# One add and one reciprocal per head, key low parts on GpSimd, first q loads on another queue

## The chip, the cores and the metric

The kernel runs on one core of a Trainium2 chip. A core has TensorE (PE, matrix products; its weight loads are shown as PEld), VectorE (DVE), ScalarE (ACT), GpSimd (POOL) and SyncE (SP), which here issues most of the DMA transfers. Each engine works through its own list of instructions in order and waits on semaphores for the others. The metric is the device time of one execution in microseconds; smaller is better.

## The reference

Attention over 4 batches, 8 heads, 576 positions and head size 64, with a mask in blocks of 64, and behind it two feed-forward layers (the second a mixture of four experts). The part that the change touches is the attention:

```python
scores = scale * np.matmul(q, k.transpose(0, 1, 3, 2))
scores = np.where(mask, scores, -1000000000.0)          # block_i >= block_j
scores = scores - np.max(scores, axis=-1, keepdims=True)
attn = np.exp(scores)
attn = attn / (np.sum(attn, axis=-1, keepdims=True) + 1e-09)
out = np.matmul(attn, v)
# then h = max(x @ w1, x @ w2, x @ w3); x = h @ w_out; then the four experts
```

## The kernel before

Heads are worked on in pairs. `load_pair` brings q, k and v of a pair; for pair 0 the transfers of q and k are cut by head, so there are four of them, k and q in turn, all issued by SP. `prep_pair` splits q and k into a rounded high part and a low part: the two 64-partition halves of `kk` hold the high part of the keys and the low part (L122, a subtraction, on VectorE), and the queries are split by L133 (ScalarE) and L135 (VectorE).

`scores(g, grp)` makes the scores of head g in two groups: group 0 holds the query blocks 0, 2 and 3 (columns of 128, 384 and 512), group 1 the block 1 (256 columns) and, in every odd head, block 4 (576 columns) for both heads of the pair. Each block goes through a row minimum from PSUM (L208, VectorE; the scores are negated) and an exponential with row sum (L215, ScalarE). At the end the function puts a closure `normalise` on a list: it adds 1e-9 to the group's sums (L223), takes reciprocals (L224), both on VectorE, and multiplies each block in place on GpSimd (L226). `stage` runs the closures of one stage behind the work of the next. `turn_probs` then transposes the blocks on TensorE (L264), in the order block 3, blocks 2 and 0, block 1, block 4; ScalarE or VectorE copy the result to `eh` (L289, L273), and `values` multiplies with v (L310, L318, L322). The result `xf` of a pair is copied by ScalarE (L327 to L334).

The heads of batch 0 run without anything beside them on TensorE. When they are done, the first layer of batch 0 (L505) fills TensorE between the heads of batch 1, and so on. The weights of that layer are converted by a chain over all engines: ScalarE L429 and L431, GpSimd L436, VectorE L438 and L439, GpSimd L443, ScalarE L85, VectorE L452, and a store L453. The rounded copies of `xf` are L523 (ScalarE) and L524 (VectorE).

The order in which instructions stand on each engine is not that of the Python text: the program is built with a scheduler that runs the instructions through a model of time and moves them, so that any edit in the attention can shift others on every engine.

Of the kernel before, what the change touches and what calls it, by code (L numbers as in the profile page):

```python
# [12 lines left out]
ALU = mybir.AluOpType  # L13
# [11 lines left out]
def program(tc, q, k, v, w123, w_out, probs, e_w1, e_w2, out):  # L25
    nc = tc.nc
# [14 lines left out]
    def f(ap):  # L41
        return ap.bitcast(F32)
# [36 lines left out]
    lo, hi, both = slice(0, 64), slice(64, 128), slice(0, P)  # L79

    QT, QW = 2 * (S - 64), 2 * S + 64
    pairs, heads, later = {}, {}, []
# [6 lines left out]
    def load_pair(g):  # L89
        b, h0 = divmod(2 * g, H)  # L90

        if g % 2:
            raw = ap_.tile([P, 2, 2, S], F32, name="raw", tag="raw")[:]
        else:
            o = (B - 1) * KD * S
            raw = arena[:, o:o + 4 * S].rearrange("p (n h s) -> p n h s", n=2, h=2)
        for hs in ((0, 1), (1, 2)) if g == 0 else ((0, 2),):
            for n, src in ((1, k), (0, q)):
                nc.sync.dma_start(out=raw[:, n, hs[0]:hs[1]], in_=src[b, h0 // 2, :, hs[0]:hs[1]])

        vraw = ap_.tile([P, 5, 2, D], F32, name="vraw", tag="vraw", bufs=4)
        nc.sync.dma_start(out=vraw, in_=v[b, h0 // 2])
        pairs[g] = dict(raw=raw, vraw=vraw)

    def prep_pair(g):


        raw, vraw = pairs[g]["raw"], pairs[g]["vraw"]
        if g < NPAIR and g % 2:

            spare = mp.tile([P, 2 * QW + 2 * S], F32R, name="spare", tag="hh")
            q1, q2 = spare[:, 0:QW], spare[:, QW:2 * QW]
            kk = spare[:, 2 * QW:].rearrange("x (h s) -> x h s", h=2)
        else:
            q1, q2 = (ap_.tile([P, QW], F32R, name=x, tag=x, bufs=1)[:] for x in ("q1", "q2"))
            kk = ap_.tile([P, 2, S], F32R, name="kk", tag="kk", bufs=1)[:]
        for x in (q1, q2):
            nc.gpsimd.memset(x[:, QT + 64:QT + 128].bitcast(U32), 0)

        def keys(hs):  # L120
            (rounded if g else lambda _, to, x: rounded(nc.vector, to, x))(nc.scalar, kk[:, hs], raw[:, 1, hs])
            nc.vector.tensor_tensor(kk[hi, hs], raw[hi, 1, hs], f(kk[hi, hs]), op=ALU.subtract)  # L122

        def queries(hs):
            x = raw[:, 0, hs]
            parts = []
            for to in (q1, q2):
                main = to[:, 0:QT].rearrange("x (h s) -> x h s", h=2)[:, hs]
                tail = to[:, QT:QW].rearrange("x (t s) -> x t s", s=64)[:, 0:3:2][:, hs]
                parts.append((main, tail))  # L130
            srcs = (x[:, :, 0:S - 64], x[:, :, S - 64:S])
            for high, src in zip(parts[0], srcs):
                nc.scalar.activation(high, src, ACTF.Copy, scale=-scale)  # L133
            for high, low, src in zip(*parts, srcs):
                nc.vector.scalar_tensor_tensor(low, src, -scale, f(high), op0=ALU.mult, op1=ALU.subtract)  # L135

        if g == 0:
            for h in range(2):
                keys(slice(h, h + 1))
                queries(slice(h, h + 1))  # L140
            yield
        else:
            keys(slice(0, 2))
            yield
            queries(slice(0, 2))
        pairs[g].update(q1=q1, q2=q2, kk=kk)
        if g < NPAIR:
            return
        vs = ap_.tile([P, 2, 5, P], F32R, name="vs", tag="vs", bufs=2)
        vh = vs[:, :, :, 0:64]  # L150
        src = vraw.rearrange("p j h d -> p h j d")
        rounded(nc.gpsimd, vh, src)
        nc.gpsimd.tensor_tensor(vs[:, :, :, 64:128], src, f(vh), op=ALU.subtract)
        pairs[g]["vs"] = vs

    GROUPS = [
        [("x", 512, [(0, 0, P), (2, P, 384)]), ("x", 512, [(3, 0, 512)])],
        [[("x", 512, [(1, 0, 256)])], [("c", 1024, [(4, 192, 576), (1, 768, 256)])]],  # L160
# [2 lines left out]
    def scores(g, grp):  # L163
# [9 lines left out]
        c0 = 3 * grp  # L173
        sets = []
        for tag, cols, plan in GROUPS[1][h] if grp else GROUPS[0]:
            st = (ps_x if tag == "x" else ps_c).tile([P, cols], F32, name="st", tag=tag)
            sets.append((st, plan))
            for i, o, w in plan:
# [5 lines left out]
                c = 0  # L184
                while c < w:
                    n = min(w - c, 512 - (o + c) % 512)
                    terms = [(part, q0, x) for q0, x in todo for part in ("q1", "q2")]
                    ends = masked and i < 4 and c + n == w
                    for m, (part, q0, x) in enumerate(terms):
                        nc.tensor.matmul(  # L190
                            out=st[:, o + c:o + c + n], lhsT=pair[part][:, q0:q0 + P],
                            rhs=pair["kk"][:, x, c:c + n], start=m == 0, stop=m == len(terms) - 1 and not ends,
                        )
                    if ends:
                        nc.tensor.matmul(
                            out=st[:, o + w - 64:o + w], lhsT=corner, rhs=corner[:, 0:64], start=False, stop=True
                        )
                    c += n
        c = c0
        done = []  # L200
        for st, plan in sets:
# [7 lines left out]
            for col, i, o, w in mine:  # L209
                x = ap_.tile([P, w], F32, name=f"p{i}", tag=f"p{i}", bufs=2 if i == 4 else 3)  # L210
# [7 lines left out]
                )  # L218
                done.append((col, x))

        def normalise():
            cs = slice(c0, c)
            nc.vector.tensor_scalar(sm[:, cs], sm[:, cs], 1e-9, None, op0=ALU.add)  # L223
            nc.vector.reciprocal(sm[:, cs], sm[:, cs])  # L224
            for col, x in done:
                nc.gpsimd.tensor_scalar(x, x, sm[:, col:col + 1], 1.0, op0=ALU.mult, op1=ALU.mult)  # L226

        later.append(normalise)


    BANKS = [
# [366 lines left out]
    for g in range(NG_):  # L598
        prep = iter(())

        n = {0: 2, 2: 3, 4: 4}.get(g) if g < H - 1 else (g + 3) // 2 if g % 2 else None
# [11 lines left out]
        b, n_pair = g // H, n  # L613
# [729 lines left out]
```

## Time and profile before

| what | value |
|---|---|
| time, median of 3 runs | 1251.9 us (1250.62 to 1252.67) |
| the profiled execution | 1249.91 us, span 1248.1 us |
| PE busy | 1211.2 us, 97% |
| DVE busy | 929.7 us, 74% |
| ACT busy | 517.8 us, 41% |
| POOL busy | 357.1 us, 29% |

The shares are averages over stages that differ. TensorE is full through most of the span, but not at its beginning: there VectorE, ScalarE and GpSimd are busier than their averages say. Stretches of time have to be read one by one.

### The profile page before, as it was taken

What the parts mean: (1) busy time and instruction counts of PE and PEld (TensorE: products, weight loads), DVE (VectorE), ACT (ScalarE), POOL (GpSimd) and SP (SyncE); (2) the same over time, 40 slices, a digit from 0 to 9 for tenths busy, and PEclk for the clock granted to TensorE, in tenths of its full rate; (3) what the DMA queues carried; (4) which work ended last, traced back from release to release, by engine and by line L of the source; (5) the groups of instructions that cost most, each with busy time, mean ns of one, the idle gap of its engine ahead of it and who ended that gap; (6) DMA issues with size and microseconds to landing.
All of it is one profiled execution on the core that took longest, in us unless ns stands there. A gap on an engine that the chain in (4) does not pass through costs nothing.

```text
span 1248.1 us, 19730 instructions
## 1 busy us (share of the span) xinstructions
PE 1211.2 (97%) x7417; PEld 1157.8 (93%) x7417; DVE 929.7 (74%) x1716; ACT 517.8 (41%) x1076; POOL 357.1 (29%) x444
## 2 busy tenths in 40 slices
PE   7879998999999999999999999999999999999998
PEld 5669997999999999989999998999999999999998
DVE  7978988666565634377888896758787888686896
ACT  7977767544544421233444441233232223322222
POOL 3957786454344212243333341000000000000000
PEclk9999999999999999999999999999999999999999
DMA  8745574554533488478887864778888887776754
GB/s 304 248 164 197 170 265 161 172 153 155 183 102 119 120 287 304 150 303 332 312 311 296 310 247 162 287 274 316 300 306 311 315 314 281 253 258 228 253 210 170
DMA packets 82644, 299.69 MB, mean 240 GB/s; under 512 B 8748, under 2 KB 18036, under 8 KB 69492
## 3 DMA queue, kind: packets, MB, share of 16 engines
q1 hardware_dynamic: 82548, 298.42, 67.3%
q8 instruction: 59, 0.97, 0.3%
q14 instruction: 37, 0.30, 0.1%
HBM read 215.26 MB, written 83.14 MB: 239 GB/s over the span
## 4 chain that ended last, share of the span: by engine, by line
PE 74%; DVE 10%; DMA 5%; POOL 4%; ACT 3%; issue 3%; SPq 0%; DVEq 0%; ACTq 0%; POOLq 0%
PE m L858 24%; PE m L505 19%; PE o L1017 17%; PE st L190 3%; PE pv L359 2%; PE o L940 2%; PE o L943 2%; PE o L944 2%; DMA t<-in_e_w 2%; PE m L1017 2%; POOL p L226 2%; PE tt L264 2%; DVE mn L208 2%; DMA part<-in_e_w 1%; POOL arena L443 1%
## 5 line engine op out<-in xcount | busy, mean ns | idle before, releaser
L505 PE MATMUL m<-xh,wt 128*128 128x288 f32 x1120 | 238.4, 298 | 0.7 <-ACT mt L541 0.4
L858 PE MATMUL m<-t,w 128*128 128x384 f32 x1152 | 228.5, 336 | 0.0
L1017 PE MATMUL o<-hx,w 128*128 128x384 f32 x1176 | 225.7, 337 | 0.0
L1017 PEld LDWEIGHTS o<-hx,w 128*128 128x128 f32 x1176 | 207.8, 188 | 0.1
L858 PEld LDWEIGHTS m<-t,w 128*128 128x128 f32 x1152 | 203.4, 188 | 2.5 <-DVE tmp L878 0.4
L505 PEld LDWEIGHTS m<-xh,wt 128*128 128x128 f32 x1120 | 183.7, 188 | 1.6 <-DVE mt L543 0.8
L858 PE MATMUL m<-b,w 128*128 128x384 f32 x864 | 175.7, 337 | 2.0 <-ACT tmp L883 2.0
L505 PE MATMUL m<-xl,wt 128*128 128x288 f32 x560 | 165.3, 295 | 0.0
L858 PEld LDWEIGHTS m<-b,w 128*128 128x128 f32 x864 | 153.2, 188 | 5.1 <-ACT tmp L883 2.3
L226 POOL TENSOR_SCALAR p<-p,sm 128x128 f32<-128x128 f32 (+1 forms) x144 | 98.7, 702 | 52.1 <-DVE sm L223 17.0
L505 PEld LDWEIGHTS m<-xl,wt 128*128 128x128 f32 x560 | 105.3, 188 | 0.3
L878 DVE TENSOR_TENSOR tmp<-m,tmp 128x384 f32<-128x384 f32 x144 | 77.9, 550 | 19.4 <-PE m L858 19.2
L505 PE MATMUL m<-hh,wo 128*128 128x288 f32 x384 | 81.3, 299 | 2.9 <-ACT arena L554 1.3
L215 ACT ACTIVATE p<-st,mn 128x128 f32<-128x128 f32 (+3 forms) x144 | 78.5, 555 | 8.2 <-DVE mn L208 6.3
L988 ACT CAST hx<-hq 128x768 fp32r<-128x768 f32 x49 | 40.6, 837 | 99.0 <-PE o L1017 75.9
L190 PE MATMUL st<-kk,q 128*128 128x128 f32 (+4 forms) x336 | 71.2, 340 | 8.7 <-ACT q L133 5.5
L940 PE MATMUL o<-w,hh 128*128 128x512 f32 x192 | 74.7, 391 | 0.9 <-ACT hh L918 0.6
L813 POOL TENSOR_TENSOR w<-part,w 128x512 fp32r<-128x512 f32 x32 | 49.2, 1557 | 91.3 <-ACT w L811 61.2
L943 PE MATMUL o<-w,hh 128*128 128x512 f32 x192 | 74.7, 390 | 0.0
L944 PE MATMUL o<-w,hl 128*128 128x512 f32 x192 | 74.1, 390 | 0.0
L543 DVE TENSOR_TENSOR mt<-m,mt 128x288 f32<-128x288 f32 x96 | 43.2, 452 | 40.3 <-PE m L505 39.9
L264 PE MATMUL tt<-ident,p 128*128 128x128 f32 x400 | 61.0, 278 | 9.8 <-POOL p L226 5.4
(169 smaller groups left out, 2173.8 us busy)
## 6 DMA issues: line engine op xcount, KB each, us to landing
w<-kb SPq DMA_DIRECT2D x55, 1024.0 KB, 6.1
w<-ka SPq DMA_DIRECT2D x30, 1792.0 KB, 7.9
ka<-w SPq DMA_DIRECT2D x16, 1792.0 KB, 6.7
wt<-held SPq DMA_DIRECT2D x54, 512.0 KB, 4.1
kb<-part SPq DMA_DIRECT2D x16, 1024.0 KB, 7.0
kb<-w SPq DMA_DIRECT2D x16, 768.0 KB, 4.7
arena<-in_w SPq DMA_DIRECT2D x18, 512.0 KB, 4.0
wo<-held SPq DMA_DIRECT2D x12, 768.0 KB, 4.5
```

The costliest lines, as they stand in the source:

```text
L190: nc.tensor.matmul(out=st[:, o + c:o + c + n], lhsT=pair[part][:, q0:q0 + P], rhs=pair["kk"][:, x, c:c + n], start=m == 0, stop=m == len(t ...
L215: nc.scalar.activation(x, st[:, o:o + w], ACTF.Exp, bias=mn[:, col:col + 1], scale=-1.0, accum_out=sm[:, col:col + 1],)
L226: nc.gpsimd.tensor_scalar(x, x, sm[:, col:col + 1], 1.0, op0=ALU.mult, op1=ALU.mult)
L264: nc.tensor.transpose(tt[:, c:c + P], pt[i][:, k0:k0 + P], ident)
L505: nc.tensor.matmul(out=out_, lhsT=w, rhs=x, start=m == 0, stop=m == n - 1)
L813: eng.tensor_tensor(w[:, a:b, 1], raw[:, a:b], f(w[:, a:b, 0]), op=ALU.subtract)
L858: ins = nc.tensor.matmul(out=m, lhsT=a, rhs=b, start=start and n == 0, stop=stop and n == 3 * KH - 1, skip_group_check=True,)
L878: nc.vector.tensor_tensor(t, x, y, op=ALU.add)
L940: ins = nc.tensor.matmul(out=o, lhsT=hh[:, ts], rhs=wh, start=i == 0, stop=False)
L943: nc.tensor.matmul(out=o, lhsT=hh[:, ts], rhs=wl, start=False, stop=False)
L944: nc.tensor.matmul(out=o, lhsT=hl[:, ts], rhs=wh, start=False, stop=i == G - 1)
L1017: nc.tensor.matmul(out=o, lhsT=a, rhs=b, start=start and m == 0, stop=stop and m == 2, skip_group_check=True,)
```

## The change

Three edits. The q transfers of pair 0 are issued by ScalarE instead of SP. The low parts of the keys of batch 0 (pairs 0 to 3, without the first head) are subtracted on GpSimd instead of VectorE. And a head's groups are normalised together: one add and one reciprocal over all of its sums, behind its second group, and the blocks are multiplied in the order in which they are transposed (3, 2, 0, then 1 or 4). The last edit holds for all 32 heads: 32 adds and 32 reciprocals go.

```diff
         for hs in ((0, 1), (1, 2)) if g == 0 else ((0, 2),):
             for n, src in ((1, k), (0, q)):
-                nc.sync.dma_start(out=raw[:, n, hs[0]:hs[1]], in_=src[b, h0 // 2, :, hs[0]:hs[1]])
+                (nc.sync if g or n else nc.scalar).dma_start(
+                    out=raw[:, n, hs[0]:hs[1]], in_=src[b, h0 // 2, :, hs[0]:hs[1]]
+                )
...
         def keys(hs):
             (rounded if g else lambda _, to, x: rounded(nc.vector, to, x))(nc.scalar, kk[:, hs], raw[:, 1, hs])
-            nc.vector.tensor_tensor(kk[hi, hs], raw[hi, 1, hs], f(kk[hi, hs]), op=ALU.subtract)
+            (nc.gpsimd if g < 4 and hs != slice(0, 1) else nc.vector).tensor_tensor(
+                kk[hi, hs], raw[hi, 1, hs], f(kk[hi, hs]), op=ALU.subtract
+            )
...
+    TURN = (2, 1, 0, 3, 4)
...
+        done = heads[g].setdefault("done", []) + done
+        heads[g]["done"] = done
+
         def normalise():
-            cs = slice(c0, c)
+            cs = slice(0, c)
             nc.vector.tensor_scalar(sm[:, cs], sm[:, cs], 1e-9, None, op0=ALU.add)
             nc.vector.reciprocal(sm[:, cs], sm[:, cs])
-            for col, x in done:
+            for col, x in sorted(done, key=lambda x: TURN.index(x[0])):
                 nc.gpsimd.tensor_scalar(x, x, sm[:, col:col + 1], 1.0, op0=ALU.mult, op1=ALU.mult)

-        later.append(normalise)
+        if grp:
+            later.append(normalise)
```

In the changed program the lines behind the edits have other numbers: L122 is L124, L190 is L195, L226 is L234, L264 is L273, L310 and L318 are L319 and L327, L436 is L445.

GpSimd at the start of the program, before (`kk` and `spare` are keys, `p` the blocks of exponentials, `arena` weights being converted):

```order
L118 MEMSET spare 128x64
L118 MEMSET q_312 128x64
L118 MEMSET q_313 128x64
L226 TENSOR_SCALAR p_167<-p_167,sm 128x128
L226 TENSOR_SCALAR p_169<-p_169,sm 128x384
L226 TENSOR_SCALAR p_172<-p_172,sm 128x512
L226 TENSOR_SCALAR p_179<-p_179,sm 128x256
L436 TENSOR_SCALAR arena<-arena 128x512
```

Head 0's multiplications came first there, in the order of the blocks; the same place in the changed program:

```order
L120 MEMSET spare 128x64
L124 TENSOR_TENSOR kk<-arena,kk 64x576
L124 TENSOR_TENSOR spare<-raw,spare 64x1152
L234 TENSOR_SCALAR p_172<-p_172,sm 128x512
L234 TENSOR_SCALAR p_169<-p_169,sm 128x384
L234 TENSOR_SCALAR p_167<-p_167,sm 128x128
L234 TENSOR_SCALAR p_179<-p_179,sm 128x256
L120 MEMSET q_303 128x64
L120 MEMSET q_304 128x64
L445 TENSOR_SCALAR arena<-arena 128x512
```

The low parts of pairs 0 and 1 now stand ahead of head 0's multiplications, and block 3 (512 columns) comes first among these.

GpSimd later, between pair 1 and pair 3, in the changed program (before, no subtraction of keys stood there):

```order
L445 TENSOR_SCALAR arena<-arena 128x512
L452 TENSOR_TENSOR arena<-arena 128x512
L124 TENSOR_TENSOR kk<-arena,kk 64x1152
L452 TENSOR_TENSOR arena<-arena 128x512
L120 MEMSET spare 128x64
L120 MEMSET spare 128x64
L234 TENSOR_SCALAR p_281<-p_281,sm 128x512
L234 TENSOR_SCALAR p_278<-p_278,sm 128x384
L234 TENSOR_SCALAR p_276<-p_276,sm 128x128
L234 TENSOR_SCALAR p_301<-p_301,sm 128x256
L124 TENSOR_TENSOR spare<-raw,spare 64x1152
L234 TENSOR_SCALAR p_382<-p_382,sm 128x512
```

The subtractions of pairs 2 and 3 stand around head 2's multiplications and ahead of head 3's.

TensorE at the end of batch 0, before: the last product of head 7 with v (`pv_903`) and the transposes of head 8 (`p_805` is its block 3, `p_802` and `p_800` its blocks 2 and 0):

```order
L310 MATMUL pv_902<-eh,vraw 128x128
L264 MATMUL tt<-ident,p_738 128x128 x2
L264 MATMUL tt<-ident,p_805 128x128 x4
L318 MATMUL pv_903<-eh,vraw 128x512 x2
L318 MATMUL pv_903<-eh,vraw 128x384
L318 MATMUL pv_903<-eh,vraw 128x256
L322 MATMUL pv_903<-eh,vraw 128x128
L264 MATMUL tt<-ident,p_802 128x128
L264 MATMUL tt<-ident,p_800 128x128
L264 MATMUL tt<-ident,p_802 128x128 x2
```

Four transposes stood ahead of the product and four behind it; in the changed program (`p_789`, `p_786`, `p_784` are the same blocks) it reads:

```order
L319 MATMUL pv_882<-eh,vraw 128x128
L273 MATMUL tt<-ident,p_724 128x128 x2
L273 MATMUL tt<-ident,p_789 128x128 x4
L273 MATMUL tt<-ident,p_786 128x128
L273 MATMUL tt<-ident,p_784 128x128
L273 MATMUL tt<-ident,p_786 128x128 x2
L327 MATMUL pv_883<-eh,vraw 128x512 x2
L327 MATMUL pv_883<-eh,vraw 128x384
L327 MATMUL pv_883<-eh,vraw 128x256
```

All eight transposes of these blocks now stand ahead of head 7's product.

## Rows read from the trace of the kernel before

**Rows 1.** The page: the span, and TensorE's busy time and share.

```profile
span 1248.1 us, 19730 instructions
...
PE 1211.2 (97%) x7417; PEld 1157.8 (93%) x7417; DVE 929.7 (74%) x1716; ACT 517.8 (41%) x1076; POOL 357.1 (29%) x444
```

**Rows 2.** Windows: length, busy us of each engine, TensorE clock, DMA, GB/s.

```profile
0.00:89.00 89.00, 69.23 (x373) 52.25 (x374) 71.98 (x144) 72.89 (x190) 58.84 (x86) 0.94 0.70 247
89.00:190.00 101.00, 99.02 (x731) 94.05 (x730) 91.76 (x202) 71.81 (x170) 79.19 (x96) 1.00 0.61 203
190.00:230.00 40.00, 34.79 (x239) 31.67 (x239) 31.21 (x78) 28.73 (x74) 24.82 (x37) 1.00 0.52 176
```

**Rows 3.** Chain of waits, 0 to 100 us: start, us, what.

```profile
11.41 1.35 DVE spare L122
...
19.96 1.50 DVE kk L122
...
31.03 2.33 DVE spare L122
...
44.55 2.29 POOL p L226 x4
```

**Rows 4.** Timeline of the first 8 us: start, us, engine, line, what, idle before.

```profile
2.12 0.43 SPq L99 DMA_DIRECT2D arena<-in_q  x1
...
4.13 0.46 DVE L87 TENSOR_SCALAR kk<-arena 128x576 fp32r<-128x576 f32 x1 [4.13 <-DMA arena<-in_k]
...
7.06 0.78 ACT L133 ACTIVATE q<-arena 128x512 fp32r<-128x512 f32 x2 [1.43 <-DMA arena<-in_q]
```

**Rows 5.** VectorE by line and shape, 0 to 100 us: busy us, mean ns.

```profile
L122 DVE TENSOR_TENSOR kk<-arena,kk 64x576 fp32r<-64x576 f32 x2 | 1.5, 755 | 0.1
...
L223 DVE TENSOR_SCALAR sm<-sm 128x1 f32<-128x1 f32 x6 | 0.8, 135 | 0.0
...
L224 DVE RECIPROCAL sm<-sm 128x1 f32<-128x1 f32 x5 | 0.8, 151 | 0.1
```

**Rows 6.** GpSimd by line and shape, whole span.

```profile
L813 POOL TENSOR_TENSOR w<-part,w 128x512 fp32r<-128x512 f32 x32 | 49.2, 1557 | 91.3 <-ACT w L811 61.2 <-PE m L858 18.7 <-PE o L944 11.4
...
L153 POOL TENSOR_TENSOR vs<-vraw,vs 128x640 fp32r<-128x640 f32 x12 | 19.4, 1617 | 0.4
```

**Rows 7.** Timeline of GpSimd and VectorE, 10 to 71 us.

```profile
16.21 2.06 POOL L226 TENSOR_SCALAR p<-p,sm 128x128 f32<-128x128 f32 x4 [2.00 <-ACT p L215]
...
30.55 1.59 POOL L443 TENSOR_TENSOR arena<-arena 128x512 int32<-128x512 int32 x1
...
31.03 2.33 DVE L122 TENSOR_TENSOR spare<-raw,spare 64x1152 fp32r<-64x1152 f32 x1
...
39.45 1.68 POOL L153 TENSOR_TENSOR vs<-vraw,vs 128x640 fp32r<-128x640 f32 x1
...
39.64 2.10 DVE L524 TENSOR_TENSOR xl<-xf,xh 128x576 fp32r<-128x576 f32 x1
...
70.46 0.76 DVE L524 TENSOR_TENSOR xl<-xf,xh 128x576 fp32r<-128x576 f32 x1 [0.69 <-ACT xh L523]
```

**Rows 8.** Timeline from 63 to 89 us, the end of batch 0.

```profile
63.24 2.96 PE L318 MATMUL pv<-eh,vraw 128*128 128x512 f32 x8
...
78.25 0.16 DVE L224 RECIPROCAL sm<-sm 128x3 f32<-128x3 f32 x1
...
78.62 2.70 POOL L226 TENSOR_SCALAR p<-p,sm 128x128 f32<-128x128 f32 x3 [1.95 <-ACT wo L85]
...
81.38 0.66 PE L264 MATMUL tt<-ident,p 128*128 128x128 f32 x4 [4.35 <-POOL p L226]
81.87 4.66 PE L318 MATMUL pv<-eh,vraw 128*128 128x512 f32 x8
...
89.00 0.38 PE L505 MATMUL m<-xh,wt 128*128 128x288 f32 x1
```

**Rows 9.** A window of 10 us, columns as in Rows 2.

```profile
80.00:90.00 10.00, 8.62 (x42) 6.21 (x43) 6.36 (x11) 6.41 (x17) 7.92 (x10) 0.83 0.65 240
```

## The prediction

> **What bounds the kernel now.** I read the page first [rows 1]. TensorE is busy for 1211.2 of 1248.1 us, so all its idle time together is 36.9 us, and no edit here takes a product away from it. The windows say where this idle time lies [rows 2]: 19.8 us (89 less 69.23) in the first 89 us, where the heads of batch 0 run alone until L505's first product [rows 8], 2.0 us from 89 to 190 us and 5.2 us from 190 to 230 us. The other 9.9 us lie behind, where the attention matters little. So the change is worth what it does to the first 89 us, and a little of the 7.2 us up to 230 us.
>
> In the first 89 us no engine is the bound alone: ScalarE is busy for 72.89 us, VectorE for 71.98, GpSimd for 58.84 [rows 2]. The chain of waits shows the turns [rows 3]: up to about 42 us it goes mostly over VectorE, with three subtractions of keys of 1.35, 1.50 and 2.33 us on it; from 44.55 us it goes over GpSimd's multiplications. It ends at the last heads, where TensorE waits 4.35 us for GpSimd at 77.0 us [rows 8].
>
> VectorE and GpSimd are not independent there. The same subtraction of 64x1152 took 1.35 us at 11.41 [rows 3], while GpSimd was still waiting for its first multiplication [rows 7], and 2.33 us at 31.03, where GpSimd's L443 ran from 30.55 to 32.14 [rows 7]. L524 took 0.76 us at 70.46 and 2.10 us at 39.64, where L153 ran until 41.13 [rows 7]. In both cases VectorE's instruction ends as if it had begun when GpSimd's was done.
>
> **The change part by part.**
>
> *The q transfers.* The last q transfer is issued at 2.12 us and ScalarE takes it up at 7.06 [rows 4]; that is where the chain begins. With the k transfers on SP and the q transfers on ScalarE, second place instead of fourth on its queue, it is issued two issues of 0.43 us earlier [rows 4]: at best -0.9 us. On ScalarE nothing but a table load stands behind them, and then work that waits for these very data. But the four transfers share the same DMA engines, and the first k, which VectorE takes up at 4.13 [rows 4], now has company from the start: I bound the loss at +0.3 and take -0.5. The Trainium skill, "DMA: Bandwidth & Descriptors", section on queues, rings and completion order, says that a DMA engine takes turns between the queues it has work for. By that rule the first k and the first q would land together, the first k later than now, and the term would be near 0; no row of before shows two queues. SP's later issues (v and pair 1) move up by the same slots, which is also company for the second q.
>
> *One add and one reciprocal.* Per head one pair of small instructions goes. Where GpSimd leaves VectorE alone the pair costs 0.135 + 0.151 = 0.29 us [rows 5]. For 8 heads this is 2.3 us of VectorE in the first 89 us, and 7 us more spread over the other 24. None of it is on TensorE's path by itself, since ScalarE is as busy as VectorE; I count 0, with 0 and -2.3 as ends. Its other side is a wait: block 3 of a head is no longer multiplied after its own group, but after both. In steady running the scores are made two heads ahead, which hides this.
>
> *The low parts of the keys.* VectorE loses 0.755 us (the second head of pair 0, [rows 5]) and 1.35, 1.50, 2.33 us [rows 3], together 5.9 us. GpSimd gains four subtractions. For them there is no row; L153 gives 1.617 us for 640 columns, 2.53 ns a column, so 1152 columns would be 2.9 us and 576 columns 1.45 us; L813 with 1557 ns for 512 columns is the upper end, 3.5 us [rows 6]. If 64 partitions cost half of 128, the lower end is 1.5 us. I take 2.9, the nearest in form. The first two (1.45 + 2.9) stand ahead of head 0's multiplications, which began at 16.21 after idle time [rows 7]: pair 1's can begin when its rounding ends, at 11.4, and is done at about 14.3, so GpSimd's idle time hides them. The other two, 5.8 us, fall between 20 and 36 us, into a stretch where each engine is busy. VectorE gets 3.83 us back there (1.50 + 2.33). The difference is 2.0 us; VectorE can go on with row minima from PSUM meanwhile, so I take half, +1.0. The ends: -3.8, if GpSimd hides all and VectorE was the bound, and +3.8 (the third rival).
>
> *The order of the multiplications.* At 78.25 the last reciprocal for head 8's first group begins, and GpSimd then does three multiplications in 2.70 us, block 3 as the last; TensorE's four transposes at 81.38 wait for that one [rows 8]. Now block 3 comes first, so these four can start about 1.8 us earlier. But the four transposes of blocks 2 and 0 now also stand ahead of head 7's product, and need the other two multiplications; the product itself so starts hardly earlier, only with 0.66 us less behind it, and I count 1.0. The reciprocal, too, stands closer behind its add: in the changed order one row minimum lies between the two, which I put at 1.0 us earlier. Together -2.0; ends 0 (both eaten by the wait for the second group's sums) and -4.35 (the whole wait).
>
> *The clock behind that wait.* TensorE idled for the 4.35 us. From 80 to 90 us the granted clock is 0.83 of full [rows 9], that is partly at 1.2 GHz, and eight products of head 7 took 4.66 us at 81.87, where those of an earlier head took 2.96 at 63.24 [rows 8]. A shorter wait may spare these 1.7 us; I take a third, -0.6, ends 0 and -1.7.
>
> *Behind 89 us.* VectorE is busy for 91.76 of 101 us from 89 to 190 [rows 2]; 0.29 us less a head gives it air, and the changed order shifts the 7.2 us of TensorE's idle time either way. I take -0.8, ends -2.5 and +2.5.
>
> The sum: -0.5 + 0 + 1.0 - 2.0 - 0.6 - 0.8 = -2.9 us. The profiled execution took 1249.9 us (span 1248.1 and 1.8 around it), which becomes 1247.0; it lies 2.0 below the median of the runs, 1251.9. From the median, I forecast 1249.0 us.
>
> **The rivals.**
>
> *More goes than I count.* Without the whole wait of 4.35 us, the 1.7 us of slow clock and the 0.9 us at the start the gain is 6.95 us: 1245.0. For it speaks that these lie behind one another on the chain; against it that the merged add makes block 3 wait for the second group.
>
> *ScalarE hides it.* ScalarE is busy for 72.89 of 89 us [rows 2], none of its computing goes, and it is in no step of the change but for two issues. If it sets the pace of batch 0, VectorE's free time turns into waiting, and only the first transfers remain: -0.5, so 1251.4. Against it speaks that the chain before 42 us goes over VectorE.
>
> *GpSimd becomes the bound: slower.* By the two pairs of rows above, a subtraction that runs on GpSimd for 2.9 us does not run beside VectorE's work on SBUF; it stops it. Then 5.8 us more of GpSimd push all that follows on its list, head 3's multiplications and the chain from 44.55 us on. The only idle time that could take it up, and that does not itself wait for VectorE, is about 2.0 us, as long as the wait at 16.21 [rows 7]. The price is +3.8: 1255.7. It decides from the point where GpSimd works without a break from pair 2's subtraction to head 5's multiplications. The Trainium skill states this mechanism in "SBUF — State Buffer", section "Who interferes with whom": VectorE with two SBUF inputs and GpSimd take turns on a shared pair of ports, and the one that comes second waits for the whole instruction. The trace agrees with 2.33 against 1.35 us. Against this rival speaks that VectorE's own subtractions, 3.8 us here, stopped GpSimd in the same way before, and that two of the four new ones fall into idle time.
>
> **How the numbers follow.** The forecast has 42 in 100, with 1247 to 1250.5 as its own range; more than I count 12; ScalarE hides it 26; GpSimd as the bound 20. About 0.2%, 2.5 us, is what a measurement of this kernel can tell from no change: faster means below 1249.4, slower above 1254.4. Of the forecast's 42 some 6 lie above 1249.4, so faster has 36 + 12 = 48; the same has 6 + 24 = 30; slower has 20 and 2 from the spread of the second rival, 22. The range reaches from the first rival's time, half a microsecond below, to the third's, a little short of it: 1244.5 to 1255.5.
>
> **What would show it.** At the start, ScalarE's second work on q before 7.06 us. GpSimd's subtraction of 64x1152 at about 2.9 us, and VectorE instructions of 2 us and more beside it, but head 0's multiplications not later than 16.2. The first product of L505, now at 89.00 us [rows 8], some 2 us earlier, the wait at 77 us about half as long, and the clock in the 10 us behind it above 0.83. I am wrong if L505 starts at 89 or later: at the same time with ScalarE without gaps, or later with GpSimd without gaps from 20 to 55 us. I am also wrong if L505 starts earlier and TensorE's idle time from 89 to 230 us grows by as much.

## The result, and the profile after

The changed kernel takes 1260.65 us (median of 6 runs, 1257.64 to 1262.32), the kernel before 1252.79 us in the same series (1250.62 to 1253.97). The ratio is 1.0063, 95% interval 1.0052 to 1.0074: 7.9 us slower, where 1249.0 was forecast, and beyond the upper end of the range, 1255.5. The profiled execution after took 1261.76 us.

The page of the changed kernel, first its span, then busy time and share of each engine:

```profile
span 1260.0 us, 19678 instructions
...
PE 1219.0 (97%) x7417; PEld 1163.9 (92%) x7417; DVE 924.8 (73%) x1648; ACT 516.4 (41%) x1076; POOL 359.7 (29%) x448
```

Against [rows 1] VectorE has 68 instructions fewer and GpSimd 4 more, as the change says. Their busy times (4.9 us less, 2.6 more) do not show by themselves what was moved, since other instructions changed with it: the four subtractions take 9.8 us on GpSimd, its multiplications 3.9 us less than before. TensorE, which has the same 7417 products, is busy 7.8 us longer; its mean granted clock is 0.991 there, 0.996 in the kernel before. The same windows as [rows 2], columns as there:

```profile
0.00:89.00 89.00, 68.49 (x353) 50.64 (x354) 67.90 (x117) 69.87 (x182) 63.90 (x84) 0.96 0.66 225
89.00:190.00 101.00, 98.06 (x725) 93.15 (x724) 89.27 (x181) 70.85 (x167) 75.20 (x100) 1.00 0.63 211
190.00:230.00 40.00, 34.46 (x213) 31.11 (x213) 33.54 (x75) 29.68 (x77) 26.50 (x33) 0.91 0.49 159
```

In each of them TensorE gets through fewer products than before. From 190 to 230 us it is busy for about as long, but at a granted clock of 0.91 instead of 1.00, and does 213 instead of 239. To see where the time went, the span is cut at four products that both kernels have. Each kernel was profiled twice, in us:

```
                              before          after         mean after - before
to the first of L505 (L514)   89.00  90.27    91.15  90.00     +0.9
to the first of L858 (L867)  430.05 429.99   435.69 435.71     +5.7
to the first of L1017        273.60 273.76   277.96 276.47     +3.5
the rest                     455.43 457.12   455.17 455.39     -1.0
span                        1248.1  1251.1   1260.0 1257.6     +9.2
```

The first 89 us, to which the prediction gave nearly all its terms, hold 0.9 of the 9.2 us. The second and the third row repeat within 0.1 and 1.5 us from one execution to the next; the loss is in the program, not in one bad run. It is idle time of TensorE and slower work at once. From the first product of L505 to the first of L858, before and then after:

```profile
89.00:519.05 430.05, 420.73 (x3110) 409.35 (x3109) 284.62 (x680) 218.15 (x530) 204.37 (x294) 1.00 0.55 180
91.15:526.85 435.70, 424.24 (x3114) 412.60 (x3114) 282.12 (x636) 218.43 (x532) 201.68 (x298) 0.99 0.55 181
```

TensorE's idle time grew from 9.3 to 11.5 us; the other 3.5 of the 5.7 us it was busy longer with the same products, at a lower granted clock. In the next stage idle time grew from 2.9 to 4.3 us and busy time from 270.7 to 273.6. In both stages together that is 3.6 us of idle time and 6.4 of slower work; between the second profiles it is 3.1 and 5.3. TensorE's waits in the first of these stages (line, waited for, us in total, times, longest): the first four after, then the first three ahead of L505 before:

```profile
PE m L514 <- ACT wo L85: 2.6, 3, 1.7
PE m L514 <- ACT arena L563: 1.9, 2, 1.3
PE m L514 <- ACT mt L550: 1.6, 3, 0.8
PE m L514 <- DVE mt L552: 1.5, 2, 1.2
```

```profile
PE m L505 <- ACT arena L554: 1.3, 1, 1.3
PE m L505 <- ACT wo L85: 1.0, 2, 0.8
PE m L505 <- ACT mt L541: 0.4, 1, 0.4
```

All waits ahead of products of L505 grew from 3.9 to 8.7 us, and those ahead of the attention's own products fell from 5.4 to 2.8, in both pairs of profiles. None of more than 0.15 us is for GpSimd's multiplications, in either kernel. Two places show how the loss comes about.

**The end of batch 1.** GpSimd, ScalarE and TensorE of the changed kernel (start, us, engine, line, what, idle before and who ended it):

```profile
189.22 0.37 ACT L220 ACTIVATE p<-st,mn 128x128 f32<-128x128 f32 x1
...
193.77 1.31 POOL L452 TENSOR_TENSOR arena<-arena 128x384 int32<-128x384 int32 x1
...
195.11 0.54 ACT L440 ACTIVATE arena<-arena 128x384 int32<-128x384 uint32 x1 [2.69 <-POOL arena L452]
195.56 0.50 ACT L85 CAST wo<-arena 128x384 fp32r<-128x384 f32 x1
...
196.11 0.40 PE L514 MATMUL m<-hh,wo 128*128 128x288 f32 x1 [1.72 <-ACT wo L85]
```

TensorE wants the next rounded piece of `wo`, ScalarE rounds it at 195.56, and ScalarE in turn waited 2.69 us for GpSimd's L452, one step of the same conversion. In the kernel before this conversion was about one piece further on:

```profile
185.23 0.37 ACT L215 ACTIVATE p<-st,mn 128x128 f32<-128x128 f32 x1
...
187.26 0.50 ACT L85 CAST wo<-arena 128x384 fp32r<-128x384 f32 x1
...
190.82 0.55 ACT L431 ACTIVATE arena<-arena 128x384 int32<-128x384 uint32 x1 [1.54 <-POOL arena L443]
191.27 0.50 ACT L85 CAST wo<-arena 128x384 fp32r<-128x384 f32 x1
```

There pieces of `wo` followed 2.0 and 6.0 us behind the head's first exponential (185.23); in the changed kernel the first of them comes 6.3 us behind it (189.22). TensorE's wait for it was 0.2 us before. The wait is followed by a fall of the clock, and so is a later one (0.84 us, for an exponential, at 218.57). The kernel before has waits here too, up to 1.33 us (at 198.1, for a copy to `eh`), and no fall. Windows of 10 us of the changed kernel, then the first of them of the kernel before:

```profile
190.00:200.00 10.00, 7.97 (x45) 6.88 (x45) 8.17 (x19) 7.30 (x20) 8.11 (x9) 0.85 0.51 159
220.00:230.00 10.00, 8.91 (x52) 8.24 (x52) 7.72 (x18) 8.32 (x22) 3.17 (x7) 0.83 0.37 128
```

```profile
190.00:200.00 10.00, 7.87 (x49) 6.65 (x50) 8.05 (x17) 8.65 (x23) 8.50 (x12) 1.00 0.31 97
```

A mean of 0.83 over 10 us means 1.7 us of lost full clock. The second profile of the changed kernel has the same wait of 1.72 us, and 0.83 from 190 to 200 us.

**The experts, behind the attention.** The same products at the same place, before and then after:

```profile
758.07 1.32 PE L858 MATMUL m<-b,w 128*128 128x384 f32 x6 [1.97 <-ACT tmp L883]
759.22 0.39 PE L940 MATMUL o<-w,hh 128*128 128x512 f32 x1
```

```profile
760.36 1.34 PE L867 MATMUL m<-t,w 128*128 128x384 f32 x6 [0.50 <-DVE tmp L887]
...
767.69 2.29 PE L867 MATMUL m<-b,w 128*128 128x384 f32 x6 [2.87 <-ACT tmp L892]
769.77 0.63 PE L949 MATMUL o<-w,hh 128*128 128x512 f32 x1
```

The granted clock there, in windows of 10 us of the changed kernel (1.00 in both in the kernel before):

```profile
760.00:770.00 10.00, 6.77 (x31) 6.46 (x32) 8.98 (x12) 3.60 (x7) 3.25 (x2) 0.85 0.59 188
770.00:780.00 10.00, 10.00 (x41) 8.60 (x41) 4.41 (x7) 0.00 (x0) 0.00 (x0) 0.81 0.24 55
```

The wait grew from 1.97 to 2.87 us, another of 0.50 us came ahead of it, and behind it the same six products took 2.29 instead of 1.32 us, and one of 512 columns 0.63 instead of 0.39: by the granted clock above, TensorE ran at 1.2 instead of 2.4 GHz for part of these 20 us. Nothing of the attention is left on TensorE there, and the change touches no line of it.

**The start.** The places of [rows 4], and GpSimd's first subtraction:

```profile
0.73 0.90 ACTq L99 DMA_DIRECT2D arena<-in_q  x2
0.74 0.87 SPq L99 DMA_DIRECT2D arena<-in_k  x2
...
5.37 0.46 DVE L87 TENSOR_SCALAR kk<-arena 128x576 fp32r<-128x576 f32 x1 [5.37 <-DMA arena<-in_k]
...
6.96 0.78 ACT L137 ACTIVATE q<-arena 128x512 fp32r<-128x512 f32 x2 [0.62 <-DMA arena<-in_q]
...
7.63 2.17 DVE L139 SCALAR_TENSOR_TENSOR q<-arena,q 128x64 fp32r<-128x64 f32 x3
7.86 1.86 POOL L124 TENSOR_TENSOR kk<-arena,kk 64x576 fp32r<-64x576 f32 x1 [6.04 <-DVE q L139]
```

The first k is taken up 1.24 us later than in [rows 4], while the last q comes only 0.10 us earlier. TensorE's first product begins at 6.77 instead of 5.54. In all profiles of this study the first k is taken up at 4.81 to 5.54 with the q loads on ScalarE's queue and at 3.54 to 4.15 without, and TensorE begins at 6.20 to 6.94 and at 5.01 to 5.57.

**The end of batch 0.** TensorE's waits in the first 91 us of the changed kernel (engine, line, waited for, us in total, times, longest):

```profile
PE st L195 <- DVE kk L124: 6.8, 1, 6.8
PE tt L273 <- DVE eh L298: 5.7, 3, 3.3
PE tt L273 <- POOL p L234: 4.5, 5, 1.5
```

The wait of 4.35 us for GpSimd [rows 8] has gone: the longest for a multiplication is 1.5 us. But all waits of the transposes for multiplications together fell only from 5.4 to 4.5 us, and TensorE now waits 5.7 us for VectorE's copies to `eh` ahead of transposes, in the kernel before 1.1 us.

### The profile page after: what moved, and what is told of

It is laid out like the page before. It is cut to its first block, busy times and chain, and to the rows that moved or that the text cites. A ratio compares the mean times of both kernels' runs of the same rounds, so it can differ in the third digit from the quotient of the medians.

```text
span 1260.0 us, 19678 instructions
## 1 busy us (share of the span) xinstructions
PE 1219.0 (97%) x7417; PEld 1163.9 (92%) x7417; DVE 924.8 (73%) x1648; ACT 516.4 (41%) x1076; POOL 359.7 (29%) x448
## 4 chain that ended last, share of the span: by engine, by line
PE 69%; DVE 12%; DMA 6%; ACT 4%; POOL 4%; issue 3%; SPq 0%; ACTq 0%; DVEq 0%; POOLq 0%
PE m L867 21%; PE m L514 18%; PE o L1026 16%; DMA t<-in_e_w 3%; PE st L195 3%; PE pv L368 2%; PE tt L273 2%; PE m L1026 2%; POOL p L234 2%; DVE mn L213 1%; DMA part<-in_e_w 1%; PE o L949 1%; PE o L952 1%; PE o L953 1%; DMA kb<-part 1%
## 5 line engine op out<-in xcount | busy, mean ns | idle before, releaser
L234 POOL TENSOR_SCALAR p<-p,sm 128x512 f32<-128x512 f32 (+2 forms) x144 | 94.6, 675 | 45.3 <-DVE sm L232 23.9
L514 PE MATMUL m<-hh,wo 128*128 128x288 f32 x384 | 84.4, 306 | 5.6 <-ACT wo L85 2.6
L195 PE MATMUL st<-kk,q 128*128 128x128 f32 (+4 forms) x336 | 70.4, 338 | 8.9 <-DVE kk L124 7.4
L273 PE MATMUL tt<-ident,p 128*128 128x128 f32 x400 | 62.3, 280 | 12.5 <-DVE eh L298 5.7
```

What stands on the lines that cost most here:

```text
L195: nc.tensor.matmul(out=st[:, o + c:o + c + n], lhsT=pair[part][:, q0:q0 + P], rhs=pair["kk"][:, x, c:c + n], start=m == 0, stop=m == len(t ...
L273: nc.tensor.transpose(tt[:, c:c + P], pt[i][:, k0:k0 + P], ident)
L514: nc.tensor.matmul(out=out_, lhsT=w, rhs=x, start=m == 0, stop=m == n - 1)
```

## The experiments

All times are medians, each ratio is to the kernel before on the same chip. The stages are those of the table above, read in each kernel's profile. "wo" is TensorE's wait for ScalarE's rounding of `wo` at one product, the 85th of L505 that takes `wo` (at 196.11 us in the changed kernel).

```
                       median   ratio  95% interval        to L505  to L858  to L1017   wo
changed kernel        1260.65  1.0063 [1.0052, 1.0074]     91.15   435.7    278.0     1.72
e1  q only            1257.18  1.0030 [1.0016, 1.0044]     98.10   431.4    273.9      -
e2  keys only         1253.93  1.0013 [1.0002, 1.0024]     91.72   427.9    274.2      -
e3  merge only        1255.67  1.0022 [1.0013, 1.0032]     90.31   432.0    275.2     1.72
e4  keys + merge      1259.90  1.0053 [1.0041, 1.0065]     90.84   435.6    278.0     1.72
e5  q + merge         1261.75  1.0071 [1.0055, 1.0087]     95.81   432.7    277.1      *
e6  q + keys          1254.25  1.0010 [0.9997, 1.0024]     91.08   429.2    275.6      -
k2  keys, 2 pairs     1253.53  1.0008 [0.9997, 1.0019]     91.77   430.2    273.6       -
o1  order only        1254.50  1.0011 [1.0001, 1.0022]     91.36   429.6    275.1       -
m0  merge, heads 0-7  1255.55  1.0023 [1.0012, 1.0033]     93.96   430.4    273.9       -
m1  merge, 8-31       1254.96  1.0013 [1.0003, 1.0023]     90.42   432.9    275.3     1.71
m3  m1 without TURN   1254.84  1.0016 [1.0005, 1.0027]     87.92   434.9    275.6     1.71
d2  no add, 8-31      1251.80  0.9996 [0.9987, 1.0005]     87.93   431.9    275.3      -
d1  one more add      1255.59  1.0018 [1.0009, 1.0027]     90.73   432.7    275.0      -
d3  no add, 0-31      1255.22  1.0017 [1.0007, 1.0027]     91.16   432.8    275.1      -
* 1.6 us for VectorE's low part of wo (L459) at another product; - no wait
```

The intervals are 1.1 to 2.0 us to either side, so a difference of two rows is uncertain by some 2 us. Each stage is read in one execution, which took between 3.0 us less (e2) and 4.2 us more (e1) than its kernel's median. In the two kernels that were profiled twice the stages repeat within 1.7 us, the one up to L858 within 0.1.

**Which of the three edits? One at a time.** The theory after the first comparison was that the late first keys and the merge cost; the rival was GpSimd as the bound.

e1, the q loads alone:

```diff
-                nc.sync.dma_start(out=raw[:, n, ...], in_=...)
+                (nc.sync if g or n else nc.scalar).dma_start(out=raw[:, n, ...], in_=...)
```

> The kernel before with the q transfers of pair 0 on ScalarE's queue alone. Theory A (the two queues share the DMA engines, so the first keys land later): VectorE takes up the first keys at about 5.4 us instead of 4.13, TensorE's first scores end at about 7.2 instead of 6.0, the loss is at least partly kept: +1.2 us (+0.5 to +2). Rival B (the loss of the change comes from the merged normalisation; the start is made up for later): the first keys as late, but the time within 0.5 us of before. Rival C (any edit makes the scheduler deal the instructions out anew, and that decides): 2 us or more to either side, with the instructions of batch 0 and 1 in another order.

e2, the keys alone:

```diff
-            nc.vector.tensor_tensor(kk[hi, hs], ...)
+            (nc.gpsimd if g < 4 and hs != slice(0, 1) else nc.vector).tensor_tensor(kk[hi, hs], ...)
```

> The kernel before with the low parts of batch 0's keys on GpSimd alone. Theory A (a subtraction on GpSimd takes about 3.3 us for 64x1152 and stops VectorE's instructions with two SBUF inputs meanwhile): +1 to +2 us, L505's first product at 90 to 91 us. Rival B (merged normalisation): within 1 us of before, or faster by up to 2, since VectorE is freed of 5.9 us. Rival C (the new order): beyond 2 us to either side.

e3, the merged normalisation with its order, alone:

```diff
+        done = heads[g].setdefault("done", []) + done
+        heads[g]["done"] = done
-            cs = slice(c0, c)
+            cs = slice(0, c)
-        later.append(normalise)
+        if grp:
+            later.append(normalise)
```

> The kernel before with one add and one reciprocal per head, and the multiplications in the order of the transposes, alone. Theory A (start and GpSimd cause the loss): -1 to +2 us. Rival B (a head's first three blocks now wait for its second group, which makes TensorE wait and its clock fall): +4 to +6 us, most of it between 90 and 235 us, with clock falls there that the kernel before does not have. Rival C (new order): beyond 2 us to either side, with no wait that names the sums or the multiplications.

The three cost 4.3, 1.0 and 2.8 us (here and below, differences of medians; the kernel before 1252.9). No single edit gains. In e1 the first keys are taken up late, as in the changed kernel, where e3 has them early:

```profile
5.12 0.46 DVE L87 TENSOR_SCALAR kk<-arena 128x576 fp32r<-128x576 f32 x1 [5.12 <-DMA arena<-in_k]
5.30 0.78 ACT L135 ACTIVATE q<-arena 128x512 fp32r<-128x512 f32 x2 [2.36 <-DMA arena<-in_q]
```

```profile
3.60 0.46 DVE L87 TENSOR_SCALAR kk<-arena 128x576 fp32r<-128x576 f32 x1 [3.60 <-DMA arena<-in_k]
4.33 0.78 ACT L133 ACTIVATE q<-arena 128x512 fp32r<-128x512 f32 x2 [2.31 <-DMA arena<-in_q]
```

In e1 k and q of head 0 are taken up 0.18 us apart instead of 0.73, the k 1.5 us later. The Trainium skill, "DMA: Bandwidth & Descriptors", section on queues, rings and completion order, says that a DMA engine takes turns between the queues it has work for; the traces agree, with these 0.18 us.

**Do they add? Two at a time.** e4, e5 and e6 are the changed kernel with one edit taken back, by the diffs above reversed.

> The changed kernel with the q transfers of pair 0 back on SP; the two other edits stay. Theory A: first keys at 4.1 us again, 1.2 us faster than the changed kernel at the start, and about +6 to +7 us against the kernel before instead of +7.9. Rival B: the same, since the start is a small part under it too; the pair that tells A from B is the keys alone against the merge alone. Rival C (new order): the time moves by 3 us or more against the changed kernel, to either side.

> The changed kernel with all low parts of the keys on VectorE again (q loads on ScalarE's queue and the merged normalisation stay). If the costs of the edits add (alone they cost +4.2, +1.2 and +2.8 us on the means), this is 1252.7 + 7.0 = 1259.7, ratio 1.0056, and the first product of L514 comes near 92 us, its start late by the first keys (VectorE takes them up near 5.2 us instead of 4.13). If the q loads cost only what they add to keys and merge (1260.65 less 1259.90 = 0.8 us), it is 1256.5, ratio 1.0030. If GpSimd with the four subtractions is what makes the merge dear (the first 89-us stage and the one behind it), it is at most 1256, and the time from the first product of L514 to the first of L867 is 433 us or less, against 435.7 in the changed kernel.

> The changed kernel with an add and a reciprocal per group again, in the order of before (q loads on ScalarE's queue and low parts on GpSimd stay). If the costs add: 1252.7 + 4.2 + 1.2 = 1258.1, ratio 1.0043, and the time from the first product of L505 to the first of L858 stays near before's 430 us, with the loss ahead of 89 us. If merge and keys are dear only together, this is near 1256.5 to 1257.2 (ratio 1.0030 to 1.0035), that is q alone. If q's loss is given back when VectorE is relieved of the keys, it is 1254 to 1255.

They do not add. The three single costs make 8.1 us, close to the 7.8 of the changed kernel (here 1260.65 less 1252.9), but only because the misses of the pairs cancel. The merge costs 2.8 us alone, but 6.0 with keys (e4 less e2), 4.6 with q (e5 less e1) and 6.4 with both (the changed kernel less e6). The q loads cost 4.3 and 6.1 us where the keys' low parts stay on VectorE (e1; e5 less e3), and 0.3 and 0.8 us where GpSimd takes them (e6 less e2; the changed kernel less e4). The keys cost 1.0 alone and 4.2 beside the merge (e4 less e3), but win 1.1 and 2.9 us beside the q loads (the changed kernel less e5; e6 less e1): 0.3 on average, which is nothing by these intervals. The merge is the only edit that costs more than the uncertainty in all four places. The rival, GpSimd as the bound, falls with e5: with the keys back on VectorE the kernel is not faster than the changed one. Nor does the loss of e4 over e3 lie where that rival has it: to L505 they differ by 0.5 us, from there to L858 by 3.6. The price of one subtraction was nearly right: 2.64 us in e2 for 1152 columns (2.9 were estimated). The two engines collide as said: the L139 group of three takes 2.17 us beside GpSimd's subtraction, where the kernel before did the same three in 0.22 and 0.83 us, and GpSimd's 576 columns take 1.86 instead of 1.41 us:

```profile
L122 POOL TENSOR_TENSOR spare<-raw,spare 64x1152 fp32r<-64x1152 f32 x2 | 5.3, 2640 | 3.7 <-ACT spare L85 3.6
...
L122 POOL TENSOR_TENSOR kk<-arena,kk 64x576 fp32r<-64x576 f32 x1 | 1.4, 1413 | 4.9 <-DVE q L137 4.9
```

k2 leaves pairs 2 and 3 on VectorE (`g < 2` instead of `g < 4`):

> The kernel before with the low parts of the keys on GpSimd for pairs 0 and 1 only, which fall into GpSimd's idle time before 16 us. Theory A (a subtraction on GpSimd costs where GpSimd is busy and VectorE waits for it): within 0.5 us of before or up to 1 us faster, against +1.4 us with all four pairs. Theory D (what costs is gaps on TensorE behind which its clock falls, and these move with any new order): the time follows the clock of the runs, not the number of subtractions.

It is not told apart from e2 or from the kernel before, so which pairs are moved can't be seen to matter.

**What of the merge costs? Order, batch 0, the rest.** o1 changes only the order of a group's multiplications, m0 and m1 merge in heads 0 to 7 and 8 to 31:

```diff
+    TURN = (2, 1, 0, 3, 4)
-            for col, x in done:
+            for col, x in sorted(done, key=lambda x: TURN.index(x[0])):
```

> The kernel before with the multiplications of each group in the order of the transposes, still one add and one reciprocal per group. Theory M (the wait for both groups costs, the order as such helps): -1 us, between -2.5 and +0.5. Theory C (a new order of the instructions, whatever it is, costs more falls of the clock): +1 to +3 us with a granted clock below 0.994 in the median.

```diff
+        merged = g < 8          # m0; g >= 8 in m1
...
-            cs = slice(c0, c)
+            cs = slice(0 if merged else c0, c)
```

> The kernel before with one add and one reciprocal per head in the 8 heads of batch 0 alone, where nothing else fills TensorE. Theory M1 (the wait for both groups costs where no product of the next layer covers it): +2 to +3 us, the whole loss of the merge alone (+2.8). Theory M2 (it costs where the heads run between the products of the first layer, from 90 to 530 us, and in the stages behind): within 1 us of before.

> The kernel before with one add and one reciprocal per head in the 24 heads of batches 1 to 3 alone. Theory M1: within 1 us of before. Theory M2: +2 to +3 us, with the first product of L505 at 89 us as before and the stretch from there to the first expert product longer than the 430 us of before.

The order, worth -2.0 us in the prediction, costs 1.6 us by itself. The merge costs 2.7 us where only batch 0 has it, by the profile ahead of the first product of L505, and 2.1 us where only the later heads have it, by the profile mostly behind it. The column "wo" separates the two.

**The merge's wait, or any new order?** Every edit here makes the scheduler move instructions on all engines, so a loss far from the edit may come from the wait that the merge adds, or from moving alone. d2 leaves the add of 1e-9 out in heads 8 to 31, which takes 48 small instructions from VectorE as m1 does, without a wait between groups; d1 adds 48; m3 is m1 with the blocks in the order of before; d3 leaves the add out everywhere. A sum that is at least 1 does not change by 1e-9 in float32.

```diff
# d2 (d3: without the condition, no add)
+            if g < 8:
                 nc.vector.tensor_scalar(sm[:, cs], sm[:, cs], 1e-9, None, op0=ALU.add)
# d1
+            if g >= 8:
+                nc.vector.tensor_scalar(sm[:, cs], sm[:, cs], 0.0, None, op0=ALU.add)
# m3: m1 with
-            for col, x in sorted(done, key=lambda x: TURN.index(x[0])) if merged else done:
+            for col, x in done:
```

> Before, with the add of 1e-9 left out in heads 8 to 31 (a float32 sum of at least 1 does not change by it): 48 small instructions less on VectorE, as many as the merge saves there, but each group is still normalised by itself. If the merge costs through block 3's wait for the second group, this has no cost: 1252.9 or a little less (ratio 0.999 to 1.000), no wait for wo over 0.5 us near 195 us, and 273.6 us from the first product of L858 to that of L1017. If the new order that the scheduler makes is the cause, it is like the merge of these heads (m1: 1255.0, ratio 1.0013), with a wait for wo of more than 1 us near 195 us or for tmp of more than 2.3 us near 762 us.

> Before, with one more add (of 0) per group in heads 8 to 31: 48 small instructions more on VectorE, 48 times 0.135 us = 6.5 us of its time. If VectorE's own time matters from 89 to 230 us, the cost is up to 2 us, and the time from L505's first product to L858's first grows from 430 to 431 or 432 us. If only the order that the scheduler makes counts, it may come out on either side, from 1251.5 to 1256, with waits of TensorE at other places. If neither, it is 1252.9.

> The merge of heads 8 to 31 with the multiplications in the order of before (blocks 0, 2, 3, then 1 or 4): block 3 waits for the second group and also stands last of its group. If the wait of block 3 for the second group is the price, it is at least as dear as m1 (1255.0), about 1255.5 to 1257 since TensorE wants block 3 first. If the order of the multiplications was what cost in m1, it is 1253 to 1254.

> Before, with the add of 1e-9 left out in all heads: VectorE has 64 small instructions less, 16 of them in batch 0 (16 times 0.135 = 2.2 us of its 72 busy us there), and nothing waits for more than before. If VectorE's time in batch 0 is on TensorE's path, the first product of L505 comes 0.5 to 2 us earlier than 89.0 to 90.3, and the whole takes 1251 to 1252.5. If the order of the scheduler is what counts, the stages move like those of the merge, to 1254 to 1256.

TensorE's longest waits from 185 to 204 us, in d2, and its only ones in m1:

```profile
PE m L506 <- POOL hh L546: 0.4, 1, 0.4
PE st L190 <- DVE kk L122: 0.4, 1, 0.4
```

```profile
PE m L512 <- ACT wo L85: 3.5, 2, 1.8
```

With as much taken from VectorE and no wait between groups there is no wait for `wo` here, and the time is that of the kernel before. Of the six kernels with the merge in heads 8 to 31, five (the changed one, e3, e4, m1, m3) wait at the product of the column "wo", 1.71 to 1.72 us, and e5 waits for the low part at another; without that merge neither the kernel before nor any of the nine others waits there. So this wait goes with the merge, in whichever order its blocks are multiplied. Waiting for `wo` does not need the merge, though: 18 products further on e1, e2 and e6 wait 1.3, 1.3 and 0.9 us for it, where m1 waits a second time (1.8 us).

That this wait is the price of the merge is not shown. m1 takes 3.2 us more than d2, but their profiles differ by 2.5 us ahead of L505, where the heads of batch 0 are the same in both, and by 1.0 from there to L858, where d2 has falls of the clock and other waits. And d1 and d3, which add no wait between groups, take as long as m1 and, from L505 to L858, 432.7 and 432.8 us to its 432.9. So the rival, that any new order of the instructions can cost this much, is not ruled out for the 2.1 us of m1; it does not explain why the merge costs in every combination, up to 6.4 us. How the merge puts the conversion a piece late inside the scheduler is not shown.

In batch 0, too, such a loss comes without the merge: d3 differs from d2 only there, by 16 instructions less for VectorE and no wait between groups, and takes 3.4 us more than d2 (L505 at 91.16 instead of 87.93). o1, too, adds nothing to any engine. Having another order at all is enough there. d1 suggests the same behind 89 us; from 320 to 510 us TensorE's longest wait is 2.8 us for a transfer that the kernel before awaits for 0.2 us (its longest there is 1.3, for ScalarE):

```profile
PE m L507 <- DMA wo<-held: 2.8, 1, 2.8
```

That VectorE's time in batch 0 is on TensorE's path is not borne out either. In d3 VectorE has 66.93 us of work up to L505 instead of 71.98, and L505 comes no earlier, at 91.16:

```profile
0.00:91.00 91.00, 70.98 (x371) 53.54 (x372) 66.93 (x125) 71.94 (x189) 59.42 (x86) 0.92 0.69 241
```

**The same kernels, profiled again.**

> The kernel before, unchanged, a second profile. It tells how far the stages move from one execution to the next: if the order of the instructions alone sets them, the first product of L505 is at 89.0 us within 0.3, the time to the first product of L858 430.0 within 0.5, and the granted clock falls at 17.2, 44.5 and 82.0 us again. If chance decides where the clock falls, these move by 1 us and more, and the clock falls in other places.

> The changed kernel, unchanged, a second profile. By the order of the instructions: first product of L514 at 91.15 us within 0.3, 435.7 us to the first of L867, clock falls at 43.4, 60.4, 197, 221 and 767 us again. By chance: other places, and stages that differ by 1 us and more.

They took 1253.12 and 1259.41 us. Behind 89 us TensorE's waits repeat to 0.3 us (in the changed kernel 1.72 for `wo`, 2.9 for `tmp` and 0.5 and 0.2 in the one ahead of it, 1.2 for `mt`; 0.2 for `wo` before). Where the clock falls repeats in part: the changed kernel had it behind the same waits near 43, 60, 197, 221 and 767 us, and once more near 19 us; the kernel before at its first and last place, longer (0.66 instead of 0.83 from 80 to 90 us), but not at 44.5 us, and its first product of L505 came 1.27 us later.

## Why the prediction was wrong

- *The q transfers, -0.5.* Wrong in sign: alone +4.3 us. The bound of +0.3 on the first k's delay was the mis-sized term; it measured 1.0 to 1.2 us. The rule of the Trainium skill that was weighed against it (together, the first k later) was the better guide, and even "near 0" was too kind: e1's profile reaches L505 9 us later, with a granted clock of 0.88 until then, 0.94 in the kernel before (this execution took 4.2 us more than e1's median). The late k is not the whole price: with the keys on GpSimd it is as late or nearly so, and the q loads cost only 0.3 and 0.8 us.
- *One add and one reciprocal, 0.* The saving is worth nothing, as said (d2: 0.9996). The wait that was weighed against it is also hidden as said, at least behind 89 us: TensorE waits there for no multiplication by more than 0.15 us in the changed kernel, and for 1.1 us in all in the worst of the others (m3). What failed is that nothing else was counted. The merge as an edit costs 2.8 to 6.4 us, through waits for weights and copies that no line of it touches.
- *The low parts of the keys, +1.0.* Right in size for the edit alone: e2 is 1.0 us slower. That is in part luck, since the same edit costs 4.2 us beside the merge and wins beside the q loads.
- *The order of the multiplications, -2.0.* The mechanism came about, the gain did not. The longest wait for a multiplication fell from 4.3 to 1.5 us, but the transposes then waited 5.7 us for copies to `eh`: all eight transposes of a head now stand together and want the copies at once. Its end of 0 was nearer, but for another reason: the prediction had the wait for the second group's sums eat the gain, the profile has the copies. The order alone costs 1.6 us (o1).
- *The clock behind that wait, -0.6.* Right at its place, wrong for the whole. From 80 to 90 us it is indeed 1.00 instead of 0.83 [rows 9]:

```profile
80.00:90.00 10.00, 6.84 (x35) 4.51 (x36) 8.57 (x15) 9.03 (x23) 8.77 (x10) 1.00 0.50 164
```

  TensorE did 35 products in it instead of 42, and the clock fell where it had been full before: 0.85 from 190 to 200, 0.83 from 220 to 230, 0.85 and 0.81 from 760 to 780 us. A fall that is spared in one place was counted as spared altogether.
- *Behind 89 us, -0.8 with 2.5 either way.* This is the step that failed most. It measured +5.7 up to L858 and +3.5 in the stage behind it. The prediction went by the idle time that was there ("the change is worth what it does to the first 89 us, and a little of the 7.2 us up to 230 us"; "The other 9.9 us lie behind, where the attention matters little"), and an order that moves can make new idle time and new falls of the clock where TensorE had been full: 3.6 us of idle time and 6.4 of slower work in these two stages. Why the scheduler's order comes out so is open.
- *The rivals.* GpSimd as the bound came nearest with its time, 1255.7, but not with its cause: the edit that it names is the cheapest of the three, 0.3 us on average. Of the two ways to be wrong that the prediction names, the first came true (L505 at 90 to 91 us, though with gaps on GpSimd), and the second in its spirit: what was lost lies behind 89 us.

How much of it is the clock? Within one kernel, over all 15 kernels, a run with a mean clock lower by 0.001 takes 0.57 us more. The changed kernel's runs had 0.9913, those of before 0.9942; by this count that goes with 1.7 of its 7.4 us (of means). For e1, e2 and e6 it is 2.4, 1.9 and 1.5 us, that is more than half of what each costs: beyond the clock, e2 and e6 are not slower than before. But the count mixes falls in batch 0, where TensorE often waits anyway, with falls behind it, where TensorE is full. For the changed kernel the profiles say more: behind 89 us its slower work (6.4 and 5.3 us) is more than its added idle time (3.6 and 3.1).

## What to carry to other kernels

On a program whose instructions a scheduler places, price an edit over the whole span: look for every wait of the bounding engine that is a microsecond or two, in stages that the edit does not touch too, and ask what each costs if it grows. Joining two small operations saves nothing on an engine that is not the bound, and in a scheduled program it moves everything else: here the joining in heads 8 to 31 cost 2.1 us, where leaving out as many instructions another way cost none, and adding some cost as much. A transfer that is put on a second queue to come earlier takes its time from the one that was first, so look whose data starts the chain.

## What the runs showed of the hardware

A subtraction of 64 partitions takes GpSimd 1.41 us for 576 columns and 2.64 for 1152, 2.3 to 2.45 ns a column, hardly less than 2.53 for 128 partitions [rows 6]: half the partitions save almost nothing. And the same wait may or may not cost the clock. m1 has the changed kernel's wait for `wo` (1.71 us, and a second of 1.8) and keeps its full clock from 190 to 200 us, where the changed kernel is granted 0.85:

```profile
190.00:200.00 10.00, 6.39 (x41) 5.07 (x40) 8.02 (x19) 7.35 (x19) 8.01 (x10) 1.00 0.42 124
```

d2 has TensorE's wait of 2.0 us in the experts like the kernel before, which kept its full clock there; in d2 it is followed by 0.83:

```profile
760.00:770.00 10.00, 10.00 (x43) 8.63 (x43) 4.52 (x8) 0.00 (x0) 0.00 (x0) 0.83 0.25 59
```

From 760 to 770 us TensorE is busy without a break in both, and does 43 products here, 53 in the kernel before.
